# Issuing five attention tiles between the row groups that make the position bias, and taking the relus off GpSimd

## The chip, the cores and the metric

The kernel runs on one core of one Trainium2 chip. The metric is the device time of one execution in microseconds (us), and less is better. The kernel before took 749.5 us, the median of 3 runs that lie between 749.07 and 752.14 us.

The engines are named as the profile names them: PE is TensorE (matmuls; PEld are its weight loads), DVE is VectorE, ACT is ScalarE, POOL is GpSimd, and SP is SyncE, which here only issues DMAs. Each works through its own instructions in the order in which they were written; an instruction that waits holds up all that stand behind it on its engine.

## The reference

Attention with a learned bias for position, then a two-layer network on its output. B = 4, H = 8 heads, S = 576, D = 64, all in float32:

```
scores = q @ k.T / sqrt(64)
x      = log1p(|i - j|) / log1p(max(i, 1))        # 576 x 576
bias   = relu(x * w1 + b1) @ w2                   # 32 hidden, 8 heads: 8 x 576 x 576
attn   = softmax(scores + bias)
y      = (attn @ v) laid out as 2304 x 512
h      = y @ w_in                                  # 2304 x 2048
out    = leaky_relu(h, 0.01) @ w_out               # 2304 x 512
```

The bias is the same for all four batches, so it is computed once and kept in DRAM.

## The kernel before

The kernel has three stages that pass into each other.

**The bias.** It is made in 36 row groups of 16 query rows; the list `GEN` says in which order. For one group (T is its number in the sequence of rows, g its place in `GEN`) there are four relu instructions over 264 to 576 columns (`gen_r`, line 111 on DVE and POOL, line 109 on ACT), matmuls that sum over the 32 hidden units (`gen_mm`, line 122), and an eviction of the result from PSUM in two ACT instructions (`gen_ev`, lines 129 and 130) into a tile `e` of which there are five. SP writes `e` to a scratch tensor in DRAM (line 141). A small planner at the top shares the relus out over ACT, DVE and POOL by assumed costs. `gen_tick(g)` issues the relus of group g+1 (those of POOL for g+3), the matmuls of g and the eviction of g-1. The rows go back to SBUF as bias tiles, in five chunks "0", "1", "M", "2" and "3", by `load_bias` (lines 162 to 168); a chunk can be loaded once its groups have been written, and SP waits for that.

**Attention.** 16 units (a pair of heads and a batch) of nine tiles each, in the order A0, B0, A1, B1, M, A2, B2, A3, B3; A0 means 128 query rows of the first head and bias chunk "0", and so on. `step(n)` issues for tile n the score matmuls (`qk_mm`, line 231), then on DVE the addition of the bias with the row maximum (line 253) and on ACT the exponential (line 254), and for tile n-3 the transposes on PE (line 291 and on) with their copies on ACT (line 307) or DVE (lines 301 and 313). After M and after B3 there is a product with v (`pv`, line 331). A product in float32 is made of a high and a low part of q and k: `split_hi` casts on DVE (lines 193 and 198), and `split_lo` subtracts on POOL (lines 205 and 208). The table `SPL` says after which tile of a unit the splits for the next unit are issued.

**The network.** Products in float32 by three matmuls each (lines 435 and 461 to 463).

The order around the change is set by the program as it is written. The loop over tiles first brings the bias as far as the table `GEN_AT` asks for before each of the first nine tiles:

```
for n in range(NTILE + LAG + 6):
    u, i = divmod(n, 9)
    if u == 0:
        while done < GEN_AT[i]:
            gen_tick(done)
            done += 1
```

With `GEN_AT = [39] * 9` all 36 groups are issued before tile A0. PSUM tiles come in three kinds, "s" (two banks each), "t" and "o" (one bank), two of each; the score tiles are "s", the transposes "t", and "o" takes the last columns of the transposes and the products with v. Row groups take "s" when they are wider than 512 columns, and otherwise "t" for an even T and "o" for an odd one.

Of the kernel before, what the change touches and what calls it, by code (L numbers as in the profile page):

```python
# [12 lines left out]
ALU = mybir.AluOpType  # L13

B, H, S, D, HID = 4, 8, 576, 64, 32
DM, DFF = 512, 2048
NT = B * S
HP = H // 2
# [6 lines left out]
KINDS = ["A0", "B0", "A1", "B1", "M", "A2", "B2", "A3", "B3"]  # L25
GEN = [16, 17] + list(range(16)) + [34, 35] + list(range(18, 26)) + list(range(33, 25, -1))
SPL = {0: [(0, "q")], 1: [(1, "q", 0)], 3: [(1, "q", 1)], 4: [(0, "k")], 5: [(1, "k", 0)], 7: [(1, "k", 1)]}
GEN_AT = [39] * 9
LAG = 3
BLK = 512  # L30
BLOCKS = [(BLK * i, min(BLK, NT - BLK * i)) for i in range((NT + BLK - 1) // BLK)]
# [4 lines left out]
def attention_ffn(ctx: ExitStack, tc: tile.TileContext, qt, kt, vm, vt, wi, wo, cst, out):  # L36
    nc = tc.nc
# [12 lines left out]
    def pstile(tag):  # L50
        shape = [128, 1024] if tag == "s" else [128, 512]
        return ps.tile(shape, F32, tag=tag, name="ps_" + tag)
# [31 lines left out]
    def gen_w(T):  # L84
        return max(S - 16 * T, 16 * T + 16)

    plan, load = [], {"a": 0.0, "v": 0.0, "p": 15.0}
    for T in GEN:
        w = gen_w(T)
        load["a"] += 0.84  # L90
        cost = {"a": 0.24 + 0.00072 * w, "v": 0.11 + 0.00056 * w, "p": 0.2 + 0.0044 * w}
        eng = ""
        for _ in range(4):
            e = min((c for c in cost if c != "p" or "p" not in eng and len(plan) >= 2), key=lambda c: load[c] + cost[c])
            load[e] += cost[e]
            eng += e
        plan.append("".join(sorted(eng, key="avp".index)))

    def gen_r(g, pool):
        T = GEN[g]  # L100
        w = gen_w(T)
        r = gr.setdefault(T, [None] * 4)
        for q, c in enumerate(plan[g]):
            if (c == "p") != pool:
                continue
            k = 4 * T + q
            t = gp.tile([128, S], F32, tag="r", name="r", bufs=13)
            if c == "a":
                nc.scalar.activation(out=t[:, :w], in_=ltw[:, :w], func=AF.Relu, bias=bps[:, k:k + 1])
            else:  # L110
                (nc.gpsimd if pool else nc.vector).tensor_scalar(out=t[:, :w], in0=ltw[:, :w], scalar1=bps[:, k:k + 1], scalar2=0.0, op0=ALU.add, op1=ALU.max)  # L111
            r[q] = t

    def gen_mm(T):
        r = gr.pop(T)
        w = gen_w(T)
        pt = pstile("s" if w > 512 else "to"[T % 2])
        cuts = [(0, w)] if w <= 512 else [(0, w // 2), (w // 2, w)]
        o0 = 512 - w // 2 if w > 512 else 0
        for a, b in cuts:  # L120
            for q in range(4):
                nc.tensor.matmul(pt[32 * q:32 * q + 32, o0 + a:o0 + b], w2d, r[q][:, a:b], start=True, stop=True)  # L122
        gps[T] = pt, o0
# [18 lines left out]

    def gen_tick(g):
        if g + 1 < 36:
            gen_r(g + 1, False)
        if g + 3 < 36:
            gen_r(g + 3, True)
        if 0 <= g < 36:
            gen_mm(GEN[g])
        if 0 <= g - 1 < 36:  # L150
            gen_ev(GEN[g - 1])
        for c in {13: "0", 28: "1", 31: "M", 38: "23"}.get(g, ()):
            load_bias(0, c)

    bias = {}

    def load_bias(hp, c):
        n = 64 if c == "M" else 128
        rows = scr[c][0:n * H * PIT].rearrange("(i h p) -> i h p", h=H, p=PIT)[:, :, 16:16 + S]
        if c == "M":  # L160
            t = ap.tile([128, S], F32, tag="biasM", name="biasM", bufs=2)
            nc.sync.dma_start(out=t[0:64, :], in_=rows[:, 2 * hp, :])
            nc.sync.dma_start(out=t[64:128, :], in_=rows[:, 2 * hp + 1, :])
        else:
            t = ap.tile([128, 2, S], F32, tag="bias", name="bias", bufs=5)
            nc.sync.dma_start(out=t[:, 0, :], in_=rows[:, 2 * hp, :])
            nc.sync.dma_start(out=t[:, 1, 64:S], in_=rows[:, 2 * hp + 1, 0:512])
            nc.sync.dma_start(out=t[:, 1, 0:64], in_=rows[:, 2 * hp + 1, 512:S])
        bias[hp, c] = t
# [3 lines left out]
    def load_unit(u):  # L173
        hp, b = divmod(u, B)
        q_, k_ = raw_b[u % 2]
        for p in (0, 64):
            nc.sync.dma_start(out=q_[p:p + 64], in_=qt[hp, b])
            nc.sync.dma_start(out=k_[p:p + 64], in_=kt[hp, b])
        raw[u] = (q_, k_)
# [292 lines left out]

    with tc.manual_schedule():
        gen_setup()
        for u in range(2):
            load_unit(u)
            load_v(u)
        sp_ops = [(u, w, a) for u in range(1) for w, a in (("q", None), ("q", 0), ("q", 1), ("k", None), ("k", 0), ("k", 1))]
        done = -1
        early_ops = []  # L480
# [6 lines that stand above are left out]
                    if done >= 6 and done % 2 == 0 and sp_ops:  # L487
                        w = sp_ops.pop(0)
                        split_hi(*w[:2]) if w[2] is None else split_lo(*w)
            if n == 8:  # L490
                gen.close()
                early = ctx.enter_context(tc.tile_pool(name="early", bufs=1, side="right"))
                x_alloc(early, 0)
                w_alloc(early, 0)
                stage, stage_y = ExitStack(), ExitStack()
                pools["s"] = stage.enter_context(tc.tile_pool(name="stage", bufs=1, side="right"))
                pools["y"] = stage_y.enter_context(tc.tile_pool(name="stage_y", bufs=1, side="right"))
            step(n)
            if n == 13:
                w_fill()  # L500
                for m in range(5):
                    early_ops += [(w_abs, m, h) for h in range(2)]
                    early_ops += [(w_bits, m, h, k) for k in range(4) for h in range(2)]
                    if m == 0:
                        early_ops += [(w_hi, 0, h) for h in range(2)] + [(w_lo, 0, h, nc.vector) for h in range(2)]
            for _ in range({0: 2, 4: 2}.get(i, 0) if n >= 18 else 0):
                if early_ops:
                    f, *args = early_ops.pop(0)
                    f(*args)
            if n == NTILE + 2:  # L510
                ffn1(0, 0)
            if u < HP * B:
                if u % B == B - 1 and u // B + 1 < HP:
                    c = {1: "0", 2: "1", 3: "M", 4: "2", 6: "3"}.get(i)
                    if c:
                        load_bias(u // B + 1, c)
                if u + 1 < HP * B:
                    for f, *args in SPL.get(i, ()):
                        (split_hi, split_lo)[f](u + 1, *args)
                if i == 4 and u + 2 < HP * B:  # L520
                    load_unit(u + 2)
                if i == 8 and u + 2 < HP * B:
                    load_v(u + 2)
# [95 lines left out]
```

## Time and profile before

| what | value |
|---|---|
| median of 3 runs | 749.5 us (749.07 to 752.14) |
| the profiled execution | 747.11 us, its span 745.3 us |
| PE busy over the span | 717.7 us, 96% |
| DVE, ACT and POOL busy | 400.0, 367.2 and 151.3 us |
| the bias, up to the last row group's eviction | 4.2 to 61.5 us |
| relus of the bias | 114 on DVE, 18 on ACT, 12 on POOL |
| mean granted clock of PE | 0.994 of full speed |

The span is the time from the first to the last instruction; 1.8 us of the execution lie outside. A busy share is not a limit by itself: matmuls are pipelined, and one that waits for its last operand in the middle of a group counts as busy. What bounds a stage is read from who waits for whom, and from the granted clock.

### The profile page before, as it was taken

What the parts mean: (1) busy time and instruction counts of PE and PEld (TensorE: products, weight loads), DVE (VectorE), ACT (ScalarE), POOL (GpSimd) and SP (SyncE); (2) the same over time, 40 slices, a digit from 0 to 9 for tenths busy, and PEclk for the clock granted to TensorE, in tenths of its full rate; (3) what the DMA queues carried; (4) which work ended last, traced back from release to release, by engine and by line L of the source; (5) the groups of instructions that cost most, each with busy time, mean ns of one, the idle gap of its engine ahead of it and who ended that gap; (6) DMA issues with size and microseconds to landing.
All of it is one profiled execution on the core that took longest, in us unless ns stands there. A gap on an engine that the chain in (4) does not pass through costs nothing.

```text
span 745.3 us, 11450 instructions
## 1 busy us (share of the span) xinstructions
PE 717.7 (96%) x4192; PEld 555.9 (75%) x4192; DVE 400.0 (54%) x1011; ACT 367.2 (49%) x797; POOL 151.3 (20%) x179
## 2 busy tenths in 40 slices
PE   6899999999999999998999999999999999999998
PEld 3236787777777777876887888888888888888896
DVE  8998778778788888848999311111211221111211
ACT  4778677876777777774555321222212222112221
POOL 2684444444354444400000000000000000000000
PEclk9999999999999999999999999999999999999999
DMA  9889839733936653102553010000100000000100
GB/s 222 260 241 263 205 86 234 162 83 112 262 88 165 164 165 91 37 22 78 177 172 110 1 56 1 1 0 1 57 0 1 0 27 31 0 1 1 57 1 29
DMA packets 30264, 68.27 MB, mean 92 GB/s; under 512 B 8192, under 2 KB 8320, under 8 KB 30208
## 3 DMA queue, kind: packets, MB, share of 16 engines
q1 hardware_dynamic: 30208, 67.54, 32.9%
q8 instruction: 33, 0.54, 0.3%
q14 instruction: 23, 0.19, 0.1%
HBM read 51.92 MB, written 15.61 MB: 91 GB/s over the span
## 4 chain that ended last, share of the span: by engine, by line
PE 80%; DVE 9%; ACT 6%; DMA 3%; issue 1%; POOL 0%; DVEq 0%; POOLq 0%; ACTq 0%
PE ps_o L435 13%; PE ps_t L435 13%; PE ps_o L331 10%; PE ps_s L461 9%; PE ps_s L462 9%; PE ps_s L463 9%; PE ps_s L231 6%; PE ps_t L291 6%; DVE p L253 3%; ACT p L254 3%; DVE r L111 3%; ACT PT L307 2%; PE ps_t L122 1%; PE ps_o L122 1%; PE ps_s L122 1%
## 5 line engine op out<-in xcount | busy, mean ns | idle before, releaser
L450 DVE TENSOR_TENSOR gl<-g,gh 128x512 fp32r<-128x512 f32 (+1 forms) x80 | 51.0, 638 | 270.5 <-ACT g L444 270.5
L231 PE MATMUL ps_s<-ks,qs 128*128 128x288 f32 x640 | 119.5, 313 | 1.5 <-DVE mx L253 1.5
L254 ACT ACTIVATE p<-p,mx 128x576 f32<-128x576 f32 x128 | 99.5, 777 | 38.3 <-DVE mx L253 21.4
L461 PE MATMUL ps_s<-woh,gh 128*128 128x512 f32 x288 | 113.7, 395 | 1.6 <-ACT g L444 1.6
L462 PE MATMUL ps_s<-wol,gh 128*128 128x512 f32 x288 | 113.9, 395 | 0.0
L463 PE MATMUL ps_s<-woh,gl 128*128 128x512 f32 x288 | 113.0, 392 | 0.5 <-DVE gl L450 0.5
L253 DVE CUSTOM_DVE_ANT_0 p<-ps_s,bias 128x576 f32<-128x576 f32 x128 | 95.0, 752 | 29.8 <-PE ps_s L231 26.8
L231 PEld LDWEIGHTS ps_s<-ks,qs 128*128 128x128 f32 x640 | 89.6, 189 | 2.9 <-DVE mx L253 2.2
L307 ACT COPY PT<-ps_t 128x512 f32<-128x512 f32 x128 | 73.4, 574 | 30.1 <-PE ps_t L291 29.9
L443 ACT ACTIVATE gh<-ps_o 128x512 fp32r<-128x512 f32 (+1 forms) x39 | 21.5, 552 | 127.8 <-PE ps_o L435 127.8
L291 PE MATMUL ps_t<-ident,p 128*128 128x128 f32 x512 | 79.5, 278 | 3.4 <-ACT PT L307 2.5
L443 ACT ACTIVATE gh<-ps_t 128x512 fp32r<-128x512 f32 (+1 forms) x39 | 21.5, 551 | 114.4 <-PE ps_t L435 114.2
L291 PEld LDWEIGHTS ps_t<-ident,p 128*128 128x128 f32 x512 | 58.5, 140 | 21.1 <-ACT PT L307 7.5
L331 PE MATMUL ps_o<-PT,v 128*64 128x288 f32 x512 | 69.2, 412 | 0.4 <-ACT PT L298 0.4
L461 PEld LDWEIGHTS ps_s<-woh,gh 128*128 128x128 f32 x288 | 54.2, 188 | 14.3 <-ACT g L444 2.0
L463 PEld LDWEIGHTS ps_s<-woh,gl 128*128 128x128 f32 x288 | 54.4, 189 | 13.6 <-DVE gl L450 1.3
L462 PEld LDWEIGHTS ps_s<-wol,gh 128*128 128x128 f32 x288 | 54.3, 189 | 11.6
L435 PE MATMUL ps_o<-xh,wil 128*128 128x512 f32 (+1 forms) x156 | 58.5, 375 | 0.0
L435 PE MATMUL ps_o<-xl,wih 128*128 128x512 f32 (+1 forms) x156 | 58.4, 375 | 0.0
L435 PE MATMUL ps_t<-xh,wil 128*128 128x512 f32 (+1 forms) x156 | 58.3, 374 | 0.0
L435 PE MATMUL ps_o<-xh,wih 128*128 128x512 f32 (+1 forms) x156 | 58.2, 373 | 0.0
L435 PE MATMUL ps_t<-xl,wih 128*128 128x512 f32 (+1 forms) x156 | 58.1, 373 | 0.0
(93 smaller groups left out, 1133.2 us busy)
## 6 DMA issues: line engine op xcount, KB each, us to landing
raw<-kt SPq DMA_DIRECT2D x32, 304.0 KB, 7.3
scr<-e SPq DMA_DIRECT2D x32, 295.5 KB, 3.4
raw<-qt SPq DMA_DIRECT2D x32, 288.0 KB, 7.0
raw<-wi SPq DMA_DIRECT2D x16, 512.0 KB, 3.8
raw<-wo SPq DMA_DIRECT2D x16, 512.0 KB, 3.6
bias<-scr SPq DMA_DIRECT2D x16, 288.0 KB, 4.1
out<-x SPq DMA_DIRECT2D x18, 256.0 KB, 2.1
v<-vm SPq DMA_DIRECT2D x16, 256.0 KB, 6.2
```

What stands on the lines that cost most here:

```text
L231: nc.tensor.matmul(s_[:, S0 + HS * hh:S0 + HS * hh + HS], qs[:, c0:c0 + 128], ks[:, k0 + HS * hh:k0 + HS * hh + HS], start=(j == 0), stop= ...
L253: nc.vector.tensor_tensor_reduce(out=p, in0=s_[:, S0:S0 + S], in1=bt, scale=-0.125, scalar=3.4e38, op0=ALU.add, op1=ALU.min, accum_out=i)
L254: nc.scalar.activation(out=p, in_=p, func=AF.Exp, bias=i, scale=-1.0, accum_out=sm_t[n][:, col:col + 1])
L291: nc.tensor.transpose(t0[:, 128 * jb:128 * jb + 128], p[:, p0 + 128 * jb:p0 + 128 * jb + 128], ident[:])
L307: nc.scalar.copy(out=PT[u, g][:, 0:8, c].rearrange("p (j h) c -> p j h c", h=2)[:, :, h, :], in_=t0[:].rearrange("p (j c) -> p j c", j=4))
L331: nc.tensor.matmul(o[64 * h:64 * h + 64, 0:HS], l, r, start=(jb == 0), stop=(jb == 4))
L435: nc.tensor.matmul(h_[:, :N], w, x[:, :N], start=(j == 0), stop=(j == len(mms) - 1))
L443: nc.scalar.activation(out=gh[:, :N], in_=h_[:, :N], func=AF.Prelu, alpha=0.01)
L450: nc.vector.tensor_sub(gl[:, :N], g[:, :N], gh[:, :N].bitcast(F32))
L461: nc.tensor.matmul(o, gh[:, c], wt[m][2][:], start=(m == 0), stop=False)
L462: nc.tensor.matmul(o, gh[:, c], wt[m][3][:], start=False, stop=False)
L463: nc.tensor.matmul(o, gl[:, c], wt[m][2][:], start=False, stop=(m == MF - 1))
```

## The change

The table `GEN_AT` now lets five tiles be issued before the last row groups: A0 after 27 of the 40 ticks (counted from -1, so that groups 0 to 25 have had their matmuls), B0 one tick later, A1 five ticks after B0, B1 one tick after A1, and M two after B1. Chunks "1", "M" and "2" are loaded seven or eight ticks sooner in the sequence. POOL makes no relus; the planner shares the 12 of them out over DVE and ACT, and 122 relus are DVE's and 22 ACT's. Odd row groups take "s" in PSUM in place of "o". The loads of unit 1 stand behind group 18 (q and k) and 33 (v), those of unit 2's q and k behind tile B3 of unit 0, and the splits for unit 1 behind tiles A2 to B3 (`SPL0`).

```diff
-GEN_AT = [39] * 9
+GEN_AT = [26, 27, 32, 33, 35, 39, 39, 39, 39]
+SPL0 = {5: [(0, "q")], 6: [(1, "q", 0), (1, "q", 1)], 7: [(0, "k")], 8: [(1, "k", 0), (1, "k", 1)]}
...
-    plan, load = [], {"a": 0.0, "v": 0.0, "p": 15.0}
+    plan, load = [], {"a": 0.0, "v": 0.0}
...
-        cost = {"a": 0.24 + 0.00072 * w, "v": 0.11 + 0.00056 * w, "p": 0.2 + 0.0044 * w}
+        cost = {"a": 0.24 + 0.00072 * w, "v": 0.11 + 0.00056 * w}
...
-        pt = pstile("s" if w > 512 else "to"[T % 2])
+        pt = pstile("s" if w > 512 else "ts"[T % 2])
...
         if g + 1 < 36:
-            gen_r(g + 1, False)
-        if g + 3 < 36:
-            gen_r(g + 3, True)
+            gen_r(g + 1)
...
-        for c in {13: "0", 28: "1", 31: "M", 38: "23"}.get(g, ()):
+        for c in {13: "0", 21: "1", 23: "M", 31: "2", 38: "3"}.get(g, ()):
             load_bias(0, c)
+        if g == 18:
+            load_unit(1)
+        if g == 33:
+            load_v(1)
...
-        for u in range(2):
-            load_unit(u)
-            load_v(u)
+        load_unit(0)
+        load_v(0)
...
-                    for f, *args in SPL.get(i, ()):
+                    for f, *args in (SPL if u else SPL0).get(i, ()):
...
-                if i == 4 and u + 2 < HP * B:
+                if i == (4 if u else 8) and u + 2 < HP * B:
                     load_unit(u + 2)
```

Three places show how it moves instructions. The line numbers of the changed kernel are one less or one more than those of the kernel before.

ACT before, from the last row groups into the first tiles (`e` are evictions, `p` exponentials; the last two rows of `e` are the last group's):

```order
L109 ACTIVATE r<-cs,bps 128x432
L129 ACTIVATE e<-ps_t,cs 128x128
L130 ACTIVATE e<-ps_t,cs 128x463
L129 ACTIVATE e<-ps_o,cs 128x144
L130 ACTIVATE e<-ps_o,cs 128x447
L129 ACTIVATE e<-ps_t,cs 128x160
L130 ACTIVATE e<-ps_t,cs 128x431
L254 ACTIVATE p,sm<-p,mx 128x576 x4
```

ACT now, at the same last groups:

```order
L255 ACTIVATE p,sm<-p,mx 128x576
L308 COPY PT<-ps_t 128x4x128
L108 ACTIVATE r<-cs,bps 128x448
L128 ACTIVATE e<-ps_s,cs 128x112
L129 ACTIVATE e<-ps_s,cs 128x479
L128 ACTIVATE e<-ps_t,cs 128x128
L129 ACTIVATE e<-ps_t,cs 128x463
L255 ACTIVATE pM,sm<-pM,mx 128x576
L308 COPY PT<-ps_t 128x4x128
L128 ACTIVATE e<-ps_s,cs 128x144
L129 ACTIVATE e<-ps_s,cs 128x447
L128 ACTIVATE e<-ps_t,cs 128x160
```

The exponentials of B1 and M, and the copies of the transposes of A0 and B0, now stand ahead of evictions of the last four groups.

DVE before, from tile M of unit 0 to tile A2 (`raw` to `ks` is the cast of k for unit 1):

```order
L253 ISA pM,mx<-ps_s,biasM 128x576
L253 ISA mx 128x1
L260 TENSOR_SCALAR sm<-sm 128x2
L261 RECIPROCAL sm<-sm 128x2
L198 CAST ks_811<-raw_81 128x1216
L253 ISA p,mx<-ps_s,bias 128x576
```

DVE now, from tile A3 of unit 0 to the first tile of unit 1 (A3, the copies of M's transposes, the cast of k for unit 1, B3, and A0 of unit 1):

```order
L254 ISA p,mx<-ps_s,bias 128x576
L254 ISA mx 128x1
L261 TENSOR_SCALAR sm<-sm 128x2
L262 RECIPROCAL sm<-sm 128x2
L302 COPY PT<-ps_o 64x2x32 x4
L199 CAST ks_894<-raw_81 128x1216
L254 ISA p,mx<-ps_s,bias 128x576
L254 ISA mx 128x1
L254 ISA p,mx<-ps_s,bias 128x576
```

The cast of unit 1's k stood ahead of A2, three tiles before the first one that reads chunk "3"; it now stands behind A3, which reads chunk "3", with one tile, B3, between it and unit 1.

## Rows read from the trace of the kernel before

**Rows 1.** The page's busy time by engine, share of the span, instructions.
```profile
PE 717.7 (96%) x4192; PEld 555.9 (75%) x4192; DVE 400.0 (54%) x1011; ACT 367.2 (49%) x797; POOL 151.3 (20%) x179
```
**Rows 2.** Busy time by stretch: from and to in us, length, then PE, PEld, DVE, ACT, POOL busy us, PE's granted clock, the DMA engines' share and GB/s. The middle and the end of the bias, the first eleven tiles, and attention further on.
```profile
13.50:47.60 34.10, 29.73 (x183) 8.60 (x178) 32.87 (x68) 22.69 (x52) 24.14 (x13) 0.95 0.86 251
47.60:59.60 12.00, 11.89 (x89) 4.27 (x84) 11.96 (x26) 9.27 (x21) 6.91 (x3) 1.00 0.90 272
59.60:76.10 16.50, 15.40 (x113) 12.11 (x110) 12.20 (x39) 13.48 (x33) 7.91 (x11) 1.00 0.97 256
90.00:120.00 30.00, 29.61 (x233) 23.34 (x232) 23.57 (x72) 22.04 (x51) 13.15 (x18) 1.00 0.48 128
```
**Rows 3.** The waits up to 60 us: us in total, times, the longest.
```profile
PEld ps_o L122 <- DVE r L111: 12.6, 31, 1.5
ACT e L129 <- DMA scrM<-e: 5.5, 2, 5.1
```
**Rows 4.** DVE while the bias is made: three rows in order of time (start, us, instructions merged with their count), and the group of all its relus (busy us, mean ns of one, idle time ahead of them).
```profile
4.17 8.74 DVE L111 TENSOR_SCALAR r<-cs,bps 128x320 f32<-128x320 f32 x23
12.83 0.75 DVE L193 CAST qs<-raw 128x1152 fp32r<-128x1152 f32 x1
...
24.89 0.79 DVE L198 CAST ks<-raw 128x1216 fp32r<-128x1216 f32 x1
...
L111 DVE TENSOR_SCALAR r<-cs,bps 128x320 f32<-128x320 f32 (+17 forms) x114 | 53.0, 540 | 1.2 <-PE ps_t L122 0.9 <-PE ps_o L122 0.3
```
**Rows 5.** Relus by shape, busy us and mean ns of one. The first two on DVE from 4 to 13.4 us, where POOL has next to nothing to do; the third and the fourth (DVE and POOL) from 13.4 to 17.1 us, beside the split of q; the fifth from 27.2 to 28.8 us, beside the split of k; the sixth from 47.2 to 55.3 us, beside relus of POOL; the last is all of POOL's relus.
```profile
L111 DVE TENSOR_SCALAR r<-cs,bps 128x512 f32<-128x512 f32 x3 | 1.3, 476 | 0.0
L111 DVE TENSOR_SCALAR r<-cs,bps 128x304 f32<-128x304 f32 x3 | 0.9, 372 | 0.0
...
L111 DVE TENSOR_SCALAR r<-cs,bps 128x496 f32<-128x496 f32 x4 | 3.9, 1041 | 0.0
L205 POOL TENSOR_TENSOR qs<-raw,qs 64x576 fp32r<-64x576 f32 x2 | 3.0, 1536 | 9.7 <-DVE qs L193 9.7
...
L111 DVE TENSOR_SCALAR r<-cs,bps 128x384 f32<-128x384 f32 x2 | 2.2, 1116 | 0.0
...
L111 DVE TENSOR_SCALAR r<-cs,bps 128x512 f32<-128x512 f32 x3 | 1.7, 601 | 0.0
...
L111 POOL TENSOR_SCALAR r<-cs,bps 128x400 f32<-128x400 f32 (+8 forms) x12 | 25.0, 2087 | 10.5 <-PE ps_t L122 6.8 <-PE ps_o L122 2.4 <-PE ps_s L122 1.2
```
**Rows 6.** ACT in order of time: the first instruction of an eviction pair, a relu, and the next pair; the end of the last eviction; then a copy of transposes, an exponential, and the next copy.
```profile
49.62 0.40 ACT L129 ACTIVATE e<-ps_o,cs 128x176 f32<-128x176 f32 x1
...
50.40 0.73 ACT L109 ACTIVATE r<-cs,bps 128x512 f32<-128x512 f32 x1
51.06 0.30 ACT L129 ACTIVATE e<-ps_s,cs 128x48 f32<-128x48 f32 x1
...
60.91 0.61 ACT L130 ACTIVATE e<-ps_t,cs 128x431 f32<-128x431 f32 x1
...
66.26 0.57 ACT L307 COPY PT<-ps_t 128x512 f32<-128x512 f32 x1
66.72 0.78 ACT L254 ACTIVATE pM<-pM,mx 128x576 f32<-128x576 f32 x1
...
67.50 0.57 ACT L307 COPY PT<-ps_t 128x512 f32<-128x512 f32 x1
```
**Rows 7.** SP in order of time (start, us of issue): the last two row groups' writes and the load of chunk "3"; the second and the fourth row are the time to landing of those writes and of that load, us.
```profile
60.55 1.66 SPq L141 DMA_DIRECT2D scr<-e  x2
DMA to landing us min/median/max: 3.6/3.7/3.9
...
65.42 0.32 SPq L166 DMA_DIRECT2D bias<-scr  x1
DMA to landing us min/median/max: 3.5/3.9/4.1
```
**Rows 8.** DVE and POOL in order of time in unit 0: the bias addition of A0, the cast of k for unit 1, A3's addition, the copies of M's transposes, and POOL's first half of the low part of k.
```profile
61.28 0.76 DVE L253 CUSTOM_DVE_ANT_0 p<-ps_s,bias 128x576 f32<-128x576 f32 x1 [1.72 <-PE ps_s L231]
66.78 0.79 DVE L198 CAST ks<-raw 128x1216 fp32r<-128x1216 f32 x1
...
69.78 0.75 DVE L253 CUSTOM_DVE_ANT_0 p<-ps_s,bias 128x576 f32<-128x576 f32 x1
...
70.74 0.93 DVE L301 COPY PT<-ps_o 64x64 f32<-64x64 f32 x4
...
69.01 1.42 POOL L208 TENSOR_TENSOR ks<-raw,ks 128x576 fp32r<-128x576 f32 x1
```
**Rows 9.** The chain that ended last, in order of time: PE from the first product with v, behind unit 1's A0, to the scores of its B0 (start, us).
```profile
72.10 2.58 PE ps_o L331 x20
74.67 0.59 PE ps_t L291 x4
...
75.48 0.54 PE ps_s L231 x4
```
**Rows 10.** PE's granted clock after a stretch in which PE had little to do; columns as in rows 2.
```profile
18.00:20.00 2.00, 0.50 (x3) 0.00 (x0) 2.00 (x7) 1.37 (x3) 0.00 (x0) 1.00 1.02 373
20.00:22.00 2.00, 1.83 (x8) 0.20 (x8) 1.12 (x4) 1.61 (x5) 0.00 (x0) 0.55 0.90 285
22.00:24.00 2.00, 1.97 (x16) 0.53 (x16) 1.65 (x4) 2.00 (x6) 1.68 (x1) 0.60 0.62 171
```

More of the change, by code (lines that the diff above doesn't have):

```diff
@@ L90, in attention_ffn, with gen_r @@
         load["a"] += 0.84
-        cost = {"a": 0.24 + 0.00072 * w, "v": 0.11 + 0.00056 * w, "p": 0.2 + 0.0044 * w}
+        cost = {"a": 0.24 + 0.00072 * w, "v": 0.11 + 0.00056 * w}
         eng = ""
         for _ in range(4):
-            e = min((c for c in cost if c != "p" or "p" not in eng and len(plan) >= 2), key=lambda c: load[c] + cost[c])
+            e = min(cost, key=lambda c: load[c] + cost[c])
             load[e] += cost[e]
             eng += e
-        plan.append("".join(sorted(eng, key="avp".index)))
-    def gen_r(g, pool):
+        plan.append("".join(sorted(eng)))
+    def gen_r(g):
         T = GEN[g]
         w = gen_w(T)
-        r = gr.setdefault(T, [None] * 4)
+        r = gr[T] = [None] * 4
         for q, c in enumerate(plan[g]):
-            if (c == "p") != pool:
-                continue
             k = 4 * T + q
@@ L110, in gen_r @@
             else:
-                (nc.gpsimd if pool else nc.vector).tensor_scalar(out=t[:, :w], in0=ltw[:, :w], scalar1=bps[:, k:k + 1], scalar2=0.0, op0=ALU.add, op1=ALU.max)
+                nc.vector.tensor_scalar(out=t[:, :w], in0=ltw[:, :w], scalar1=bps[:, k:k + 1], scalar2=0.0, op0=ALU.add, op1=ALU.max)
             r[q] = t
```

## The prediction, made before the changed kernel was run

> **What bounds the kernel now.** Read the page's busy times first [rows 1]: PE is busy for 96% of the span, so time is won only where PE has too little to do, or where its work starts sooner. The stretches [rows 2] show where that is. From 90 us on PE is busy for 29.61 of 30 us; a delay or a gain at the start is carried through to the end there. While the bias is made, up to 59.6 us, DVE is the engine without a gap (11.96 of 12.00 us in the second stretch), and the waits [rows 3] say the same from PE's side: its weight loads for one kind of PSUM tile alone wait 12.6 us for relus of DVE. From 59.6 us to the first tiles of unit 1 no engine is full: PE 15.40, ACT 13.48 and DVE 12.20 of 16.50 us. So the change touches two things: DVE's relus, and the passage from bias to attention, in which PE loses about 1 us. What must not come later is the point where unit 1's second tile has its scores, 76.02 us (75.48 + 0.54) [rows 9]; behind it PE's order of work is the same in both kernels.
>
> **DVE up to the first tile.** Alone on its ports DVE did its first 23 relus in 8.74 us, 0.380 each [rows 4], where a single one is recorded with 0.372 us for 304 columns and 0.476 for 512 [rows 5], 0.0005 us a column; successive ones overlap by some 0.08 us. The 114 relus before have 439 columns in the mean, by the plan, so they would need 0.364 us each, 41.5 in all. They took 53.0 us [rows 4]: 11.5 us of stretch. It comes with POOL's work. Beside the split of q four relus took 1.041 us each where 0.47 is the price alone: 2.3 us lost; beside the split of k 1.116 in place of 0.41, for some four again: 2.8 us [rows 5]. Those 5.1 us stay. The other 6.4 us go with POOL's relus (25.0 us of them), beside which a 512-wide relu takes 0.601 in place of 0.476 [rows 5]. The 1.2 us in which DVE waited for PE [rows 4] go too: they follow from the 5.1 us in which ACT's eviction waited for a write [rows 3], behind the loads of unit 1, which are no longer there.
>
> The Trainium skill ("SBUF — State Buffer", Who interferes with whom) has it that whichever of the two engines takes the shared ports first holds them for its whole instruction and the other is blocked in full. The trace agrees only in part: beside the subtractions it comes near to that (2.3 us lost beside 3.0 us of POOL), beside 25.0 us of relus it does not (6.4 lost). By the rule the four splits would cost some 6.1 us in place of 5.1 and the sum below would come out 1 us higher.
>
> Against the gain, 122 relus now stand on DVE, 8 more. Tile A0 is issued behind the relus of 27 groups: 92 relus in the new plan, 423 columns in the mean, 0.356 us each, 32.7 us; with the two casts (0.75 and 0.79, [rows 4]) and 5.1 us of stretch, from 4.17 us: DVE is there at 43.5 us. Before, the relus of these groups were done at 47.6 us (the point from which 26 relus follow up to 59.6 us [rows 2]; the last nine groups have 27). A gain of 4.1 us at this point.
>
> **The last ten groups with five tiles between them.** Before, they took from 47.6 to 61.52 us (60.91 + 0.61, the last eviction [rows 6]), 13.9 us. Now ACT has to do, in that order: 11 pairs of evictions at 0.78 (49.62 to 50.40), 8.6 us; 6 relus at 0.55 to 0.65 (50.40 to 51.06 for a wide one), 3.5; five exponentials at 0.78 (66.72 to 67.50), 3.9; two copies at 0.46 (66.26 to 66.72), 0.9 [rows 6]. That is 16.9 us. ACT is no longer ahead of its tiles: an exponential waits for DVE's addition (0.76), the addition for the scores, and the scores for a PSUM tile that an eviction has to free; from the end of the last relu to the first addition 1.72 us went by [rows 8]. I find three places where ACT stands idle: ahead of A0's exponential, of A1's (its scores take the bank of a group whose eviction stands just ahead on ACT) and of M's, some 1.2 us each (an addition and half of those 1.72), 3.6 in all. So the last eviction ends at 43.5 + 16.9 + 3.6 = 64.0 us, 2.5 us later than before: five tiles inside the bias take more than DVE has won. Bounds: without any of the three waits 60.4, with twice of them 67.6. I take the middle, since in the last 12 us of the bias DVE and PE are full and ACT is busy for 9.27 us [rows 2].
>
> **The wait that takes over.** Chunk "3" can be loaded when the last group is written. Before, 3.9 us lay between the last eviction's end and the issue of that load (61.52 to 65.42), and it landed 3.5 to 4.1 us after [rows 7]: at some 69.2 us, just ahead of A3's addition at 69.78 [rows 8]. Five tiles that needed no such load covered it. Now only A2 and B2 stand between. The load is issued at 64.0 + 3.9 = 67.9 and lands at 71.7 us, and A3's addition starts there, held up for some 5 us. Behind it on DVE stand its own 0.68, maximum and reciprocals (0.28, to 70.74), four copies, 0.93, and then the cast of unit 1's k, 0.79 [rows 8]: 2.7 us. POOL's low half of k follows, 1.42 [rows 8], and only then PE can finish unit 1's first scores, some 0.4 us more. From there PE's chain is that of before, 72.10 to 76.02, 3.9 us [rows 9]. Sum: 71.7 + 2.7 + 1.4 + 0.4 + 3.9 = 80.1 us against 76.0: 4.1 us later. Before, the cast stood at 66.78 us, ahead of A2, and none of this was on the path.
>
> **PE's clock.** PE has nothing left from about 67 us, when A2 to B3 have their scores and the transposes that can be made, until the cast of k at 74 us. Before, a stretch in which PE was busy for 0.50 of 2 us was followed by 4 us with a granted clock of 0.55 and 0.60 [rows 10]: 3.4 us of them at the lower of the two levels, 1.2 GHz. That costs (0.45 + 0.40) x 2 = 1.7 us of PE's time, and in the chain of scores, products and transposes after the gap PE sets the pace. Bounds: 0 (the clock stays up), 3.4 (twice as long). I take 1.7, the one case in the rows.
>
> **Edits at nothing.** The loads of unit 2's q and k stand behind chunk "3" on SP in both kernels. The earlier loads of chunks "1", "M" and "2" land ticks before their tiles. With odd groups in "s" there are four PSUM tiles in use for bias in place of six; an eviction one group behind, as now, leaves room. If that cover fails, ACT's waits above grow; it is in their upper bound. The load of unit 1 behind group 18 competes with the writes of `e`, of which five can be under way before ACT has to wait; if that is not enough, it is the third rival below.
>
> **The sum.** 4.1 + 1.7 = 5.8 us later than the profiled 747.11 us: 752.9 us. The median of the runs shown is 749.5 us, 2.4 us above that execution; the forecast for the median is 749.5 + 5.8 = 755.3 us.
>
> **Rivals.** First, the same chain with less in it: the three waits of ACT do not show and the clock stays up. Then the last eviction ends at 60.4, chunk "3" lands at 68.1, and unit 1's second tile is 4.1 - 3.6 = 0.5 us later than before: 750.0 us. For it speaks that ACT has gaps before, which more work could fill; against it that the order on ACT ties evictions to tiles.
>
> Second, faster: POOL's relus held up more than the relus of DVE show, and the splits' stretch goes with them. If all of the 11.5 us goes, DVE is at A0 5.1 us sooner, at 38.4 us; the last eviction ends at 38.4 + 20.5 = 58.9 us and chunk "3" lands at 66.6, where 67.6 (71.7 - 4.1) is break-even: 1.0 us gained, and 4.6 without the three waits as well. From a last eviction before 59.9 us on the change gains. Near the upper end, 4 us, that is 745.5 us. Against it: the splits are still there, and beside them the relus were slowest.
>
> Third, slower still: the load of unit 1 in the middle holds up the writes of `e` as the loads at the start did before, where ACT lost 5.1 us [rows 3]. Then the last eviction comes that much later: 755.3 + 5.1 = 760.4 us. Against it: there two units' loads stood ahead of the writes, here one does.
>
> **Chances.** The forecast 0.55, from 753 to 758 us; the first rival 0.30, the second 0.08, the third 0.07. A change of under 0.5% (3.75 us) cannot be told from none. Of the forecast nearly all lies above 753.25 us, which makes 0.61 for slower with the third rival; 0.31 for the same, the first rival and a rest; 0.08 for faster. The range reaches from 748 us, just under the first rival, to 760.
>
> **What would show it.** Right: DVE's additions of A0 at 43 to 45 us; relus of 500 columns near 0.47 us wherever POOL is idle; the last eviction after 61.5 us; DVE idle for some 5 us ahead of A3's addition with a DMA of the bias named; PE idle for several us at 67 to 74 us, and a granted clock under 1 after it. Wrong: A3 starting without a wait, or unit 1's second tile with scores before 76 us. The relus of the first 9 us should read as before.

## The result, and the profile after

The changed kernel takes 757.88 us, the median of 4 runs (756.73 to 761.86); the kernel before, on the same chip, 749.29 (748.0 to 752.14). That is a ratio of 1.0131 with a 95% interval of 1.010 to 1.0162: 9.8 us more, 7.5 to 12.1. The two medians themselves lie 8.6 us apart. The forecast was 755.3 us and a loss of 5.8 us, likeliest slower. The direction came, and the time lies within the range; but the loss is larger than forecast by more than the measurement's uncertainty. The profiled execution took 757.86 us, its span is 755.8 us.

The page's busy times, which answer to [rows 1], and its row of PE's score matmuls: 5.8 of the 11.6 us in which PE stood idle ahead of them end with the cast of unit 1's k, the chain that the prediction has behind chunk "3":

```profile
PE 717.1 (95%) x4192; PEld 557.7 (74%) x4192; DVE 395.7 (52%) x1019; ACT 368.8 (49%) x801; POOL 127.0 (17%) x167
...
L232 PE MATMUL ps_s<-ks,qs 128*128 128x288 f32 x640 | 122.3, 318 | 11.6 <-DVE ks L199 5.8
```

PE does the same work, 717 us, in a span 10.5 us longer. The stretches, to be read beside [rows 2], show where it stood still (columns as there: five busy times, then the granted clock, the DMA engines' share and GB/s):

```profile
13.50:44.00 30.50, 25.98 (x176) 9.89 (x168) 29.24 (x71) 21.15 (x48) 6.13 (x4) 1.00 0.80 224
44.00:64.00 20.00, 15.42 (x117) 6.84 (x118) 14.62 (x40) 16.33 (x37) 0.44 (x1) 0.83 0.83 266
64.00:80.00 16.00, 9.42 (x60) 6.54 (x59) 8.26 (x26) 8.15 (x20) 7.22 (x8) 0.83 0.82 215
...
90.00:120.00 30.00, 28.49 (x224) 22.68 (x220) 22.88 (x72) 21.24 (x51) 13.70 (x18) 1.00 0.30 82
```

Up to 42.7 us DVE has no gap, and POOL does its four subtractions and no more. From 44 to 64 us no engine is full, from 64 to 80 us PE is busy for 9.42 of 16 us, and from 90 us on it is nearly full again. DVE in order of time, where the rows of A0's and A3's additions answer to [rows 8]:

```profile
24.08 18.65 DVE L110 TENSOR_SCALAR r<-cs,bps 128x400 f32<-128x400 f32 x49
46.66 0.76 DVE L254 CUSTOM_DVE_ANT_0 p<-ps_s,bias 128x576 f32<-128x576 f32 x1 [3.92 <-PE ps_s L232]
...
74.05 0.76 DVE L254 CUSTOM_DVE_ANT_0 p<-ps_s,bias 128x576 f32<-128x576 f32 x1 [4.47 <-DMA bias<-scr]
...
75.95 0.80 DVE L199 CAST ks<-raw 128x1216 fp32r<-128x1216 f32 x1
...
84.19 0.76 DVE L254 CUSTOM_DVE_ANT_0 p<-ps_s,bias 128x576 f32<-128x576 f32 x1 [3.26 <-PE ps_s L232]
```

The relus of 27 groups end at 42.73 us (24.08 + 18.65). Then come two stops. At A0's addition DVE waits 3.92 us for scores; at A3's it waits 4.47 us for the load of a bias. Unit 1's second tile is added at 84.19 us (the last row), where before it was 76.05: 8.1 us late. ACT, with the last eviction that answers to [rows 6], says where the first stop comes from:

```profile
44.86 0.46 ACT L128 ACTIVATE e<-ps_s,cs 128x240 f32<-128x240 f32 x1 [4.18 <-DMA scrM<-e]
...
67.29 0.64 ACT L129 ACTIVATE e<-ps_t,cs 128x431 f32<-128x431 f32 x1
```

An eviction waits 4.18 us for a write of an `e` tile, and A0's scores stand behind that eviction's bank. On SP, in order of time, the writes for chunk "M" stand behind the four loads of unit 1, and the load of chunk "3", which answers to [rows 7], at 71.20 us:

```profile
35.56 0.59 SPq L178 DMA_DIRECT2D raw<-qt  x1
...
37.48 0.59 SPq L179 DMA_DIRECT2D raw<-kt  x1
38.17 1.87 SPq L140 DMA_DIRECT2D scrM<-e  x2
...
71.20 0.33 SPq L167 DMA_DIRECT2D bias<-scr  x1
```

And PE behind the second stop: it is idle for 5.79 us, then once more for POOL's half of k, and the 20 products with v take 3.68 us (79.07 to the next transposes at 82.75) where [rows 9] have 2.58:

```profile
76.89 0.82 PE L232 MATMUL ps_s<-ks,qs 128*128 128x288 f32 x2 [5.79 <-DVE ks L199]
78.29 0.85 PE L232 MATMUL ps_s<-ks,qs 128*128 128x288 f32 x2 [0.58 <-POOL ks L209]
79.07 3.26 PE L332 MATMUL ps_o<-PT,v 128*64 128x288 f32 x16
82.17 0.65 PE L332 MATMUL ps_o<-PT,vt 128*64 128x288 f32 x4
82.75 0.66 PE L292 MATMUL ps_t<-ident,p 128*128 128x128 f32 x4
```

From there the delay is carried along: tile M of unit 1 is added at 88.57 us in place of 80.43, tile M of unit 7 at 190.41 in place of 182.26, both 8.1 us later. Between 200 and 213 us this execution lost another 2.4 us; the profiles of most experiments did not, so it is left out of the account of the change. So the loss is 8.1 us by the traces at that point, 8.6 by the medians and 9.8 by the ratio.

### The profile page after: what moved, and what is told of

Same layout as the page of the kernel before. It is cut to its first block, busy times and chain, and to the rows that moved or that the text cites. A ratio compares the mean times of both kernels' runs of the same rounds, so it can differ in the third digit from the quotient of the medians.

```text
span 755.8 us, 11454 instructions
## 1 busy us (share of the span) xinstructions
PE 717.1 (95%) x4192; PEld 557.7 (74%) x4192; DVE 395.7 (52%) x1019; ACT 368.8 (49%) x801; POOL 127.0 (17%) x167
## 4 chain that ended last, share of the span: by engine, by line
PE 72%; DVE 16%; ACT 7%; DMA 3%; issue 1%; SPq 0%; POOL 0%; DVEq 0%; ACTq 0%; POOLq 0%
PE ps_o L436 11%; PE ps_t L436 11%; PE ps_o L332 11%; PE ps_s L463 8%; PE ps_s L462 8%; PE ps_s L464 8%; PE ps_s L232 6%; PE ps_t L292 5%; DVE p L254 3%; ACT p L255 3%; DVE r L110 3%; ACT PT L308 2%; PE ps_s L121 2%; DVE tmp L406 2%; DVE tmp L408 2%
## 5 line engine op out<-in xcount | busy, mean ns | idle before, releaser
L232 PE MATMUL ps_s<-ks,qs 128*128 128x288 f32 x640 | 122.3, 318 | 11.6 <-DVE ks L199 5.8
L232 PEld LDWEIGHTS ps_s<-ks,qs 128*128 128x128 f32 x640 | 91.4, 192 | 17.1 <-issue 10.2
L332 PE MATMUL ps_o<-PT,v 128*64 128x288 f32 x512 | 70.8, 420 | 0.4 <-ACT PT L299 0.4
L463 PEld LDWEIGHTS ps_s<-wol,gh 128*128 128x128 f32 x288 | 54.4, 189 | 11.6
L265 POOL COPY rb<-sm 128x128 f32<-128x128 f32 x80 | 30.5, 381 | 171.7 <-DVE sm L262 160.0
```

The source lines that it names most:

```text
L232: nc.tensor.matmul(s_[:, S0 + HS * hh:S0 + HS * hh + HS], qs[:, c0:c0 + 128], ks[:, k0 + HS * hh:k0 + HS * hh + HS], start=(j == 0), stop= ...
L332: nc.tensor.matmul(o[64 * h:64 * h + 64, 0:HS], l, r, start=(jb == 0), stop=(jb == 4))
L463: nc.tensor.matmul(o, gh[:, c], wt[m][3][:], start=False, stop=False)
```

## The experiments

My theory after the result: the change consists of a gain and a loss. The relus without GpSimd win some 4 us on DVE. Against that, the tiles between the groups cost more, in three terms of one chain: ACT's wait for a write at 45 us, the wait for chunk "3" with too few tiles to cover it, and what is queued behind A3 (the cast and half of k, and a slower clock). The rivals are that GpSimd was of no harm, and that some of these waits are hidden by others. The edit that puts odd row groups into "s" in PSUM was not tried by itself; it is in every run with tiles between the groups.

Ratios are to the kernel before on the same chip in the same set of runs, with 95% intervals; 0.001 is 0.75 us. Times of different sets are compared by these ratios. Line numbers differ a little between kernels.

**One half of the change each: e1 and e2.** e1 has the planner's and `gen_r`'s part of the diff alone, e2 all the rest.

```
e1:  before, with
-        cost = {"a": 0.24 + 0.00072 * w, "v": 0.11 + 0.00056 * w, "p": 0.2 + 0.0044 * w}
+        cost = {"a": 0.24 + 0.00072 * w, "v": 0.11 + 0.00056 * w}
e2:  changed kernel, with gen_r and the plan of before
```

> Of the change only the planner's part: no relu on GpSimd, all else as before (no tile between the groups, both units loaded at the start). My theory: DVE has 122 relus of 0.364 us, two casts (1.54) and the 5.1 us that the splits cost, from 4.17 us on: its last relu ends at 55.2 us, or 56.4 if it still waits 1.2 us for PE, where the kernel before has 59.6. All that follows moves with it: 3.2 to 4.4 us sooner than before, so 745 to 746 us. Rival: ACT, which waits for the writes behind the loads of unit 1, sets the end of the bias and not DVE; then the relus end sooner, but the last eviction stays near 61.5 us and the time within 1 us of before. Second rival: the two GpSimd subtractions alone explain the stretch of DVE, and the 8 additional relus make it 2 to 3 us slower.

> Of the change only the order of issue: five tiles between the last ten groups, the bias loads and unit 1's loads and splits moved as in the changed kernel, but GpSimd keeps its relus and the planner is that of before. My theory: the two parts of the change have opposite signs, so this one loses more than both together: DVE comes to tile A0 some 4 us later than in the changed kernel (47 in place of 43 us) and the time is 3 to 5 us above it, 761 to 763 us. Rival: GpSimd takes relus from ACT too, which is the full engine in the last ten groups; then the tail gets shorter by what DVE comes later, and the time is that of the changed kernel, 757 to 759 us.

e1: 744.99 us, ratio 0.9953 (0.9932 to 0.9973), 3.5 us less than before. e2: 757.48 us, ratio 1.0118 (1.0092 to 1.0145), 8.8 us more. For e1 the theory held, as two rows of DVE show: the last run of relus ends at 54.88 us (33.90 + 20.98), where 55.2 was expected and before has 59.6.

```profile
33.90 20.98 DVE L109 TENSOR_SCALAR r<-cs,bps 128x560 f32<-128x560 f32 x59
56.61 0.76 DVE L249 CUSTOM_DVE_ANT_0 p<-ps_s,bias 128x576 f32<-128x576 f32 x1 [1.74 <-PE ps_s L227]
```

For e2 the theory fell: it is as slow as the changed kernel, not 3 to 5 us slower, although DVE does come later. Rows of DVE and ACT in e2:

```profile
37.72 8.68 DVE L112 TENSOR_SCALAR r<-cs,bps 128x304 f32<-128x304 f32 x21
48.02 0.76 DVE L258 CUSTOM_DVE_ANT_0 p<-ps_s,bias 128x576 f32<-128x576 f32 x1 [1.63 <-PE ps_s L236]
...
46.24 0.46 ACT L130 ACTIVATE e<-ps_s,cs 128x240 f32<-128x240 f32 x1 [3.61 <-DMA scrM<-e]
```

The relus end at 46.40 us, 3.7 later than in the changed kernel, but ACT waits for the same write up to 46.24 us, so A0 is only 1.4 us later (48.02 against 46.66). Most of one half's gain is lost in the wait that the other half brings. How much of it was that, and how much the rival (GpSimd spares ACT), e2 alone does not tell; e5 does.

**The wait for a write: e3 and e5.**

```
e3:  changed kernel, with
-    e = gp.tile([128, S + 15], F32, tag="e", name="e", bufs=5)
+    e = gp.tile([128, S + 15], F32, tag="e", name="e", bufs=8)
e5:  e2 with the same edit
```

> The changed kernel with eight buffers for the evicted rows in place of five, so that ACT need not wait for a write that stands behind unit 1's load. My theory: the 4.18 us in which ACT waits for a write at 45 us go, tile A0's exponential and the evictions behind it come that much sooner, and as the load of chunk 3 is the end of this chain, the whole gain is carried on: 3 to 4 us less than the changed kernel, 754 to 755 us. Rival: the writes themselves are late (SP issues them behind the load of a chunk), so the loads of chunks come no sooner, and the time is within 1 us of the changed kernel although ACT no longer waits there.

> As e2 (GpSimd keeps its relus), with eight buffers for the evicted rows: the same pair as changed kernel and e2, but without ACT's wait for the write at 45 us, behind which DVE's being late may have hidden. My theory: the relus of GpSimd cost DVE some 3.7 us up to tile A0 (46.4 against 42.7 us in e2 and the changed kernel), and without that wait nothing hides it: 3 to 4 us above e3, about 756 us. Rival: GpSimd's relus spare ACT as much as they cost DVE, and the time is within 1 us of e3's, 752 to 753 us.

e3: 752.44 us, ratio 1.0055 (1.0037 to 1.0074), 4.1 us more than before, so by the ratios 5.7 of the 9.8 us are gone, by the medians 4.0 of 8.6. e5: 755.82 us, ratio 1.0095 (1.0071 to 1.0119), 3.0 us above e3. Both went the way that the theory had, e3 by more than its 3 to 4 us in the ratios; as the intervals are wide, and those of e3 and e5 touch, the sizes are better read from the traces. In e3 DVE reaches A0 without a stop, and all that follows, A3's wait among it, stands 3.5 us earlier than in the changed kernel:

```profile
29.75 12.93 DVE L110 TENSOR_SCALAR r<-cs,bps 128x368 f32<-128x368 f32 x39
42.96 0.76 DVE L254 CUSTOM_DVE_ANT_0 p<-ps_s,bias 128x576 f32<-128x576 f32 x1 [0.29 <-PE ps_s L232]
...
70.48 0.76 DVE L254 CUSTOM_DVE_ANT_0 p<-ps_s,bias 128x576 f32<-128x576 f32 x1 [4.44 <-DMA bias<-scr]
...
80.77 0.76 DVE L254 CUSTOM_DVE_ANT_0 p<-ps_s,bias 128x576 f32<-128x576 f32 x1 [3.42 <-PE ps_s L232]
```

In e5 the relus end at 46.30 us (33.64 + 12.66), A0 is added 3.6 us later than in e3, and unit 1's second tile 3.2 us later:

```profile
33.64 12.66 DVE L112 TENSOR_SCALAR r<-cs,bps 128x560 f32<-128x560 f32 x28
...
83.97 0.76 DVE L258 CUSTOM_DVE_ANT_0 p<-ps_s,bias 128x576 f32<-128x576 f32 x1 [4.04 <-PE ps_s L236]
```

So GpSimd's relus do cost some 3 us. e2's rival holds for a small part only: behind A0 ACT has one relu fewer in e5 than in e3 (5 against 6), and from A0's addition to the last eviction's end 20.4 us go by in place of 21.4.

Eight tiles remove the wait in e3. That the loads of unit 1 made the write late was not tried by moving them in the changed kernel, but the traces bear it out. The two writes for chunk "M" take 3.2 us from issue to landing in before, where no load stands just ahead of them, and 6.0 to 6.6 us in the changed kernel. There the load of chunk "1" is issued right behind them, at 40.75 us, and could be a cause too. But e11 (further on) has the loads of unit 1 ahead of the same writes, at 33.25 us, and the load of chunk "1" only at 45.95 us, and there the writes take 7.5 to 7.8 us. So the load of chunk "1" is not needed for it. The time to landing of the two writes in before, the changed kernel and e11:

```profile
DMA to landing us min/median/max: 3.2/3.2/3.2
DMA to landing us min/median/max: 6.0/6.3/6.6
DMA to landing us min/median/max: 7.5/7.7/7.8
```

**What is queued behind chunk "3": e4 and e6.**

```
e4:  changed kernel, with
-SPL0 = {5: [(0, "q")], 6: [(1, "q", 0), (1, "q", 1)], 7: [(0, "k")], 8: [(1, "k", 0), (1, "k", 1)]}
+SPL0 = {5: [(0, "q"), (0, "k")], 6: [(1, "q", 0), (1, "q", 1), (1, "k", 0), (1, "k", 1)]}
e6:  e4, with bufs=8 for e
```

> The changed kernel with unit 1's k cast and its low half made beside those of q, two tiles sooner, ahead of tile A3's addition. My theory: what stands between the landing of chunk 3 and unit 1's first scores falls from the addition, four copies, cast and GpSimd half to the addition alone: PE resumes at some 74.9 in place of 76.9 us and has no second wait of 0.6 us, so 2 to 3 us less than the changed kernel, 755 to 756 us. Rival: PE's order (transposes and products of unit 0 that wait for A3's and B3's copies) sets the pace behind the gap, and the time is within 1 us of the changed kernel.

> The edits of e3 and e4 together. My theory: both lie on one chain, one ahead of chunk 3's load and one behind it, so their gains add: 5 and 2 us less than the changed kernel, 750 to 751 us. It stays above before, since A3's addition still waits some 4 us for the load of chunk 3 and A0 to A2 lie ahead of the last groups on ACT. Rival: with both gone the tiles between the groups pay, and the time falls under that of before by a further 2 us or more, to 746 us or less.

e4: 755.7 us, ratio 1.0098 (1.0069 to 1.0127); e6: 749.9 us, ratio 1.0003 (0.9985 to 1.0021). By the ratios e4 is 2.5 us under the changed kernel, as expected, but the intervals overlap. The trace is sharper, as ACT's wait before it varies (5.18 us in e4's profile): from A3's addition to that of unit 1's second tile there are 7.95 us (75.57 to 83.52, the rows below) in place of 10.14 in the changed kernel, 2.2 us less.

```profile
75.57 0.76 DVE L254 CUSTOM_DVE_ANT_0 p<-ps_s,bias 128x576 f32<-128x576 f32 x1 [4.01 <-DMA bias<-scr]
...
83.52 0.76 DVE L254 CUSTOM_DVE_ANT_0 p<-ps_s,bias 128x576 f32<-128x576 f32 x1 [1.93 <-PE ps_s L232]
```

In e6 both gains add up, a little more than expected, to the time of before, and not below it. Between e6 and e1 there are still 3.7 us; e10 and e12 look into them.

**PE's clock: e8 and e9.** Both add 24 matmuls on a constant (48 instructions) whose result nobody reads; e8 into a bank of its own ahead of unit 1's first scores, e9 into columns of B3's bank that its scores leave free.

```
e8:  changed kernel, with
+            if n == 9:
+                d = pstile("t")
+                for _ in range(24):
+                    nc.tensor.matmul(d[:, 0:128], ident[:], ident[:], start=True, stop=True)
             step(n)
e9:  changed kernel, with
         st[n] = s_
+        if n == 8:
+            for _ in range(24):
+                nc.tensor.matmul(s_[:, 0:128], ident[:], ident[:], start=True, stop=True)
```

> The changed kernel with 24 matmuls of 128 columns on constants, whose result nobody reads, issued on PE ahead of unit 1's first scores, where PE is idle for 5.8 us. My theory: the granted clock fell to 0.83 for this gap and the stretch behind it; with PE at work in it, the clock of that stretch rises toward 1.00, the 20 products behind the gap take 2.6 in place of 3.7 us, and the time is about 1 us less than the changed kernel, 756 to 757 us. Rival: the clock falls for the gaps between 44 and 64 us, not for this one; then the products stay at 3.7 us and the time is that of the changed kernel or, if the added matmuls outlast the gap, above it.

> As e8, but the 24 matmuls on constants go into the free columns of tile B3's score bank, right behind B3's scores, so that they need no bank for which PE has to wait: they run inside the gap, from some 70 us on. My theory: PE is then busy for some 5 of the 5.8 us ahead of unit 1's first scores, the granted clock behind the gap stays at or near 1.00, the 20 products take 2.6 in place of 3.7 us, and the point where unit 1's tile M is added comes about 1 us sooner than in the changed kernel (87.5 in place of 88.6 us); the time is 1 us less, 757 us. Rival: the clock behind the gap is low all the same, from the idle time between 44 and 64 us, and that point does not move.

e8: 760.93 us, ratio 1.0153 (1.0133 to 1.0173). It did not test what it was meant to: its matmuls waited for a bank of M's transposes and ran behind the gap, from 78.05 us on. Its row of PE and, in the second fence, its stretches still show the clock:

```profile
78.05 8.00 PE L501 MATMUL ps_t<-ident 128*128 128x128 f32 x48 [5.25 <-ACT PT L299]
```

```profile
76.00:80.00 4.00, 1.95 (x9) 1.95 (x10) 3.15 (x11) 2.07 (x5) 1.72 (x3) 0.53 1.00 233
80.00:84.00 4.00, 4.00 (x25) 4.00 (x25) 0.00 (x0) 0.66 (x3) 1.49 (x1) 0.62 1.02 278
84.00:90.00 6.00, 6.00 (x51) 4.61 (x50) 1.72 (x5) 1.11 (x3) 2.12 (x2) 1.00 1.03 289
```

e9: 756.37 us, ratio 1.011 (1.0087 to 1.0133). Here PE worked through the gap, and the same 48 instructions took 5.52 us in place of 8.00. Its row of PE, its stretches, and, last, the same stretches of the changed kernel:

```profile
72.40 5.52 PE L237 MATMUL ps_s<-ident 128*128 128x128 f32 x48
```

```profile
76.00:80.00 4.00, 2.86 (x24) 2.41 (x22) 3.35 (x11) 1.83 (x5) 1.48 (x2) 1.00 1.05 239
80.00:84.00 4.00, 3.72 (x29) 2.33 (x29) 1.84 (x5) 1.78 (x5) 2.14 (x4) 1.00 1.03 261
```

```profile
76.00:80.00 4.00, 2.52 (x8) 1.54 (x10) 2.33 (x6) 1.58 (x4) 2.91 (x2) 0.50 1.01 219
80.00:84.00 4.00, 4.00 (x29) 2.53 (x26) 0.89 (x3) 1.43 (x3) 2.12 (x2) 0.83 1.04 382
```

The clock is 1.00 where it was 0.50 and 0.83, that is, it stayed at 2.4 GHz. The point that I had named did not come sooner (tile M of unit 1 at 89.14 us), because in this profile ACT's wait at 45 us was 5.25 us and A3's addition 2.0 us later. From A3's addition to unit 1's second tile there are 8.72 us (76.04 to 84.76), 1.4 less than in the changed kernel. So the gap's clock costs 1.4 us. The medians agree in sign (1.6 us by the ratios), though their intervals overlap.

**What GpSimd's subtractions cost: e7 and e11.**

```
e7:  e1, with
     def split_lo(u, what, a):
+        eng = nc.gpsimd if u else nc.vector
...
-            nc.gpsimd.tensor_sub(dst, q_[64:128, S * a:S * a + S], dst.bitcast(F32))
+            eng.tensor_sub(dst, q_[64:128, S * a:S * a + S], dst.bitcast(F32))
...
-            nc.gpsimd.tensor_sub(ks2[:, c], k_[:, c], ks1[:, c].bitcast(F32))
+            eng.tensor_sub(ks2[:, c], k_[:, c], ks1[:, c].bitcast(F32))
e11: e7, with bufs=8 for e, load_unit(1) and load_v(1) behind groups 18 and 33
```

> e1 with the low halves of unit 0's q and k made by DVE in place of GpSimd. My theory: DVE loses some 5 us of its relus beside these four GpSimd subtractions; made by DVE itself they cost four instructions of 0.4 to 0.75 us, some 2.5 us in all, and nothing beside them is stretched: the last relu ends 2 to 3 us sooner and the time is 1 to 3 us less than e1's, 742 to 744 us. Rival: the stretch lies with DVE's own casts or with the loads and writes that run at that time, and the relus stay as slow: then it is 2.5 us slower than e1, 747 to 748 us.

> No tile between the groups; no relu and no low half of unit 0 on GpSimd (as e7); eight buffers for the evicted rows, and unit 1's loads behind the groups 18 and 33, as in the changed kernel, so that no write stands behind them at the start. My theory: in e7 DVE's relus no longer stretched, but ACT waited 8.25 us for a write and DVE 4.29 us for PE behind it, which took back what was won; without that wait the last relu ends at 53 to 54 us and A0's addition stands at 55 us, where e1 has 56.6 and e7 58.8: 742 to 743 us, the fastest of all. Rival: DVE's wait comes from PE or the banks themselves, and the time stays at e7's 744 to 745 us.

e7: 744.67 us, ratio 0.9942 (0.9923 to 0.9961); e11: 742.17 us, ratio 0.9922 (0.9901 to 0.9944), the fastest of all. e7 gave nothing that can be told from e1, but the relus did what was expected; DVE and ACT in e7:

```profile
13.53 2.77 DVE L109 TENSOR_SCALAR r<-cs,bps 128x496 f32<-128x496 f32 x7
16.33 0.76 DVE L202 TENSOR_TENSOR qs<-raw,qs 64x576 fp32r<-64x576 f32 x1
...
24.85 1.15 DVE L109 TENSOR_SCALAR r<-cs,bps 128x432 f32<-128x432 f32 x3 [4.29 <-PE ps_t L120]
...
21.46 0.70 ACT L127 ACTIVATE e<-ps_s,cs 128x528 f32<-128x528 f32 x1 [8.25 <-DMA scrM<-e]
```

Without GpSimd's work seven relus took 2.77 us, 0.40 each, where [rows 5] have 1.041 beside it. But DVE, being faster, ran into the wait of ACT for a write behind the loads of unit 1, and stood still for 4.29 us. e11 takes that wait away, but for 0.83 us at 43.46 us, by two edits at once, more buffers and later loads: the relus end at 52.53 us (29.79 + 22.74) and A0's addition is at 54.25 us.

```profile
29.79 22.74 DVE L109 TENSOR_SCALAR r<-cs,bps 128x336 f32<-128x336 f32 x64
54.25 0.76 DVE L254 CUSTOM_DVE_ANT_0 p<-ps_s,bias 128x576 f32<-128x576 f32 x1 [1.73 <-PE ps_s L232]
```

**The cover for chunk "3": e10 and e12.**

```
e10: e6, with
-GEN_AT = [26, 27, 32, 33, 35, 39, 39, 39, 39]
+GEN_AT = [26, 27] + [39] * 7
e12: e10, with
-        if g == 33:
+        if g == 38:
             load_v(1)
```

> e6 with two tiles (A0 and B0) between the groups in place of five. My theory: what is left of the loss in e6 is cover: five tiles ahead of the last groups put their exponentials and waits before the last eviction on ACT, and leave two tiles only to cover the load of chunk 3. With three tiles fewer the last eviction ends some 4 us sooner (three exponentials of 0.78 and two waits of 1.2 us) and five tiles stand behind it, so A3's addition no longer waits: 2 to 4 us less than e6, 746 to 748 us. Rival: the three tiles cost behind the groups what they cost between them, and the time is within 1 us of e6, 749 to 751 us.

> e10 with unit 1's v loads issued behind the load of chunk 3 in place of ahead of the last three writes. My theory: in e10 the cover came (five tiles behind the last eviction, which ended 58.0 us), but SP issued the last three writes only at 60.9 us, behind the v loads from 57.95 us on, while the DMA engines were full, and chunk 3 was loaded 8 us after the last eviction in place of 3.3. Without the v loads ahead of them the writes are issued 2 to 3 us sooner and chunk 3 is loaded at 62 to 64 us: A3's wait falls from 4.2 to 1 or 2 us and the time to 745 to 747 us, 1 to 3 us less than e10. Rival: the DMA engines are full in any case and the writes land no sooner: the time stays within 1 us of e10's, 748 to 749 us.

e10: 748.11 us, ratio 1.0006 (0.9991 to 1.0021), the same as e6: its rival was right. e12: 746.68 us, ratio 0.9986 (0.9974 to 0.9998), 1.5 us under e10, though the intervals overlap. In e10 the last eviction ends at 57.98 us, 6.5 us sooner than in e6, and three more tiles stand behind it. Yet A3 waits as long, since the load comes late; SP and DVE in e10:

```profile
57.95 0.79 SPq L185 DMA_DIRECT2D v<-vm  x1
58.79 2.01 SPq L187 DMA_DIRECT2D vt<-vt  x2
60.90 1.91 SPq L140 DMA_DIRECT2D scr<-e  x3
65.99 0.33 SPq L167 DMA_DIRECT2D bias<-scr  x1
...
68.97 0.76 DVE L254 CUSTOM_DVE_ANT_0 p<-ps_s,bias 128x576 f32<-128x576 f32 x1 [4.23 <-DMA bias<-scr]
```

From the last eviction to the load there are 8.0 us, where the changed kernel has 3.3 (67.93 to 71.20). Part of it are the loads of v ahead of the last three writes, as e12 shows: 6.7 us (57.64 to 64.34), and A3 waits 2.73 us. Beside the rest stand DMA engines that are busy for 0.96 of the time from 56 to 60 us in e10 and e12, and for 0.80 and 0.51 from 64 to 68 and 68 to 72 us, around the last writes of the changed kernel; that this is its cause was not tried. What does decide is when the load is issued: with the load 1.65 us sooner (64.34 against 65.99) A3 is added 1.7 us sooner (67.27) and the time falls by 1.5. With e1 2.5 us faster still, what the two tiles between the groups cost beyond that stays open.

## Why the prediction was right, and where it was not

**DVE up to the first tile.** Right. 43.5 us was forecast, 42.73 came; GpSimd's relus cost DVE 3.7 us (e2, e5), near the 4.1 of the sum. The subtractions beside the relus took their part too: e7's relus ran at 0.40 us without them. The Trainium skill ("SBUF — State Buffer", Who interferes with whom) has it that, of the two engines on the shared ports, the one that comes second is blocked in full. The trace comes near to that beside the subtractions (2.3 us lost beside 3.0 in before); beside GpSimd's relus it does not. Up to the first tile e2 has 19.4 us of them (25.52 us of GpSimd from 13.5 to 44 us, 6.13 of them the subtractions). DVE was 3.7 us later there with 87 relus than the changed kernel with 92, so the stretch is an estimated 5.5 us (3.7, and five relus at the 0.356 of the sum).

**The last ten groups.** The step that failed is the sentence in "Edits at nothing" that costs the moved load of unit 1 at nothing, and the weight of 0.07 on the third rival, which is the same mechanism. ACT waited 4.18 us for a write (4.18 to 5.25 over the profiles with five tiles `e`), and A0's addition, forecast at 43.5 us, came at 46.66. e3 removes this wait and nothing else: its last eviction ends at 64.38 us, where 64.0 was forecast (A0 0.5 us sooner, and 21.4 us behind it in place of 20.5), and its time is 4.1 us above before, where 5.8 was forecast. So the working of this part held with the wait left out, the three waits of 1.2 us among it (in the changed kernel ACT idles 0.90, 1.29 and 1.51 us ahead of the exponentials of A0, A1 and M). The rival's size was 5.1 us; by e3 it is 5.7 in the ratios, whose intervals reach 2.3 and 1.4 us to each side, 4.0 in the medians and 3.6 at A3's addition (74.05 against 70.48).

**The wait that takes over.** Right in kind. Chunk "3" was loaded 3.3 us after the last eviction (3.9 forecast), A3's addition waited 4.47 us (5 forecast), and the cast and POOL's half of k stood behind it, worth 2.2 us by e4. But from the last eviction's end to A3's addition there are 6.1 us (67.93 to 74.05, and as many in e3), where 7.7 was forecast (64.0 to 71.7): 1.6 too many.

**PE's clock.** Right in kind: 1.7 us forecast, 1.4 measured by e9. From A3's addition to unit 1's second tile the sum had 10.1 us (71.7 to 80.1, and 1.7 of the clock); the changed kernel took 10.14.

**The sum.** Two misses of opposite sign met in it. Unit 1's second tile was forecast 5.8 us late and came 8.1 us late: the last eviction ended 3.9 us later than forecast (67.93 against 64.0), 3.6 of it by the wait for the write, as e3 shows, and the way from there to A3's addition took 1.6 us less. That the time came as near to the forecast as it did is in part luck. With the third rival's 5.1 us on top of the forecast it would have been 10.9 us, where the ratio gives 9.8 and the medians 8.6. The forecast and this rival belonged together: the forecast took the wait at the start away, with the loads that made it, and did not charge the wait that one of these loads makes where it was put.

**The signs that were named.** One failed: A0's addition came at 46.66 us and not at 43 to 45, again by the wait for the write. The others came: relus of 496 columns at 0.466 us with GpSimd idle, the last eviction after 61.5 us, a DMA of the bias ahead of A3, PE idle for 5.79 us and a lower clock behind it.

**The other rivals.** The first, no difference, needed ACT's waits and the clock to be hidden; both showed. The second, faster by the rest of DVE's stretch, fails because the subtractions were still there (6.13 us of GpSimd from 13.5 to 44 us). Freed of them, with eight tiles `e` and the loads of unit 1 later, and without tiles between the groups, e11 gains 5.8 us.

## What to carry to other kernels

When work is moved into a stage that waits for transfers, follow each load that moves with it to the buffers of the queue behind it: here the wait for a write that stood behind four loads cost about as much as the relus taken off GpSimd won (3.6 us at A3's addition, against some 3). When a load can start only at the end of a stage, let nothing that could be ready earlier queue behind its consumer (2.2 us in e4). Keeping more work behind that stage as cover pays only if the load itself comes no later: e10 gained nothing by three more tiles of it. Measure two edits apart before adding them up: half of this change alone is 3.5 us faster than before, and inside the whole its gain could not be seen.

## What was not expected of the hardware

PE's clock did not come back as soon as PE was busy. In e8 it was idle from 72.8 to 78.05 us, and the granted clock of its single microseconds fell to 0.50 (1.2 GHz) within that time. PE then worked without a gap and was still granted 0.50 up to 83 us, and 0.97 to 1.00 behind it. The price of a gap is thus on the work behind it: idle time that looks free at the end of a wait is paid for after the wait.

The time from a last write to the load that depends on it is not a constant. From the last eviction to the load of chunk "3" it was 3.9 us in before, 3.3 in the changed kernel, 3.2 in e3, and 6.7 and 8.0 in e12 and e10, where the DMA engines were busy for 0.96 of the time from 56 to 60 us.
